# Another written order of the first group of an attention and MoE kernel

## The chip, the cores and the metric

One core of a Trainium2 chip. The metric is the device time of one execution, in microseconds (us), lower is better. The engines are TensorE (PE, with its weight loads PEld), VectorE (DVE), ScalarE (ACT), GpSimd (POOL) and SyncE (SP, which here only issues DMAs); each runs its own instructions in order, and they meet through semaphores.

## The reference, cut to what matters

Attention over 4 batches, 8 heads, 576 positions and 64 columns a head, half of the heads with a plain window of 32, half with a window of 128 at stride 4; then two MoE-like blocks on the 2304 tokens.

```python
scores = scale * q @ k.T            # per batch and head, then masked by window
attn = exp(scores - max) / sum
x = (attn @ v)                      # -> 2304 tokens x 512
h = x @ w_in                        # 512 -> 2048
x = (h - tanh(h)) @ w_out           # 2048 -> 512
a, b = x @ w1, x @ w2               # 512 -> 1024
out = ((a * b) @ w3) @ w_out2       # 1024 -> 1024 -> 512
```

## The kernel before, in words

Every fp32 product is done as three products of a high part and a low part of each operand. The hidden dimension of the first MoE block is worked in four groups of 3, 4, 4 and 5 chunks of 128 columns; after it come w1, w2, w3 and the output. **The change touches only the first group**, in which attention, the conversion of the first weights and the first products of the MoE block are interleaved. Their order is one written string, `ORDER` (lines 49 to 69), which `first_group` (line 756) walks through word by word. Each word emits the instructions of one step on one engine (or one queue), so the string sets the order on every engine at once. The rest of the program is emitted by loops and is not in the string.

A word is a letter, a number, and for attention mostly a `p` (plain heads) or `d` (dilated heads). The number of an attention word is the unit, 0 to 11 (three units of 192 positions a batch). From unit 3 on some steps do both halves at once. The attention words, in the order in which one unit goes through them:

- `q` (load_q, line 425): two loads of k and q on SP, 576 to 608 KB a half; `v` (load_v, line 444): two or three loads, 384 KB a half.
- `s` (at_scores, line 480): TensorE, mask and 48 small products a half, each 32 columns wide on the output side (tile `s`).
- `M` (at_max, 522): VectorE, a maximum and a subtraction; `E` (at_exp, 533): ScalarE; `N` (at_norm, 537): VectorE, a sum (L541), an addition (L545) and a reciprocal (L546); `m` (at_mult, 548): GpSimd.
- `T` (at_T, 557): TensorE, three transposes (tile `t`, one PSUM buffer); `C` (at_Tcopy, 568): ScalarE, two copies (L574).
- `P` (at_pv, 579): TensorE, 24 products with v for a half, 64 columns wide on the output side (L592, tile `x`, two PSUM buffers); `X` (at_hi, 611): ScalarE, high part (L614); `L` (at_lo, 616): VectorE, low part (L619).

The weight words go through weights 0 to 13 in the order in which they are needed:

- `w`: a load of 512 KB on SP into the tile `st`, which has two buffers (so the load of weight n+2 is issued only when the steps of weight n are done with its buffer);
- `a` (cv_abs, 142): ScalarE, L144; `b` and `c` (cv_bits, 147): VectorE, two instructions each (L149, L153; L159, L162); `i` (cv_hi, 166): ScalarE, L167; `o` (cv_lo, 169): GpSimd, L170.

The words of the MoE block go through 24 steps (seven tiles of 256 tokens and one of 512, three chunks each), and step 24 of the next group: `h` (st_h, 652) is 12 products of TensorE into the one PSUM buffer `h`, `t` (tanh, ScalarE, L677), `g` (VectorE, L683, which frees that buffer), `G` (ScalarE, L690), `k` (GpSimd, L697), `y` (st_y, 709: 12 products of TensorE, L725), and after a tile's last `y` the copies out, `Y` on ScalarE and `Z` on VectorE. `h0` needs the first three plain units and the three dilated halves up to `L1d`. K prepares masks, Q closes the pools of attention.

So what sets the order of work around the change is the string alone, and behind it four in-order engines and one in-order queue (SP). A wait of one word on an engine holds all later words of that engine. Three tiles with few buffers tie them together: `st` (2), `h` (1) and `s` (1 from unit 3 on, freed by `M`).

```python
            if kind in of_rest:
                of_rest[kind](n)
            elif part in "pd":
                of_unit[kind](n, ("pd".index(part),))
            else:
                of_unit[kind](n)
```

Of the kernel before, what the change touches and what calls it, by code (L numbers as in the profile page):

```python
# [46 lines left out]


ORDER = """
w0 K0 K1 a0 b0 c0 q0p q1p q2p q0d q1d s0p s1p w1 M0p M1p E0p E1p s2p M2p N0p N1p m0p w2 q2d s0d E2p  # L50
M0d a1 v0p v1p v2p N2p v0d b1 m1p E0d T0p c1 m2p s1d C0p T1p C1p a2 M1d P0p T2p X0p P1p s2d E1d w3
L0p C2p X1p N0d N1d m0d T0d C0d P2p a3 m1d T1d b2 X2p L1p P0d M2d q3p q3d v1d b3 c2 C1d E2d X0d i0
i1 N2d L2p s3 L0d q4p P1d m2d X1d c3 v2d i2 T2d C2d L1d q4d w4 M3 o0 w5 h0 t0 P2d g0 E3 N3 X2d o1 h1
q5p s4 o2 i3 G0 t1 g1 o3 L2d v3p k0 h2 a4 y0 q5d G1 a5 t2 b4 k1 c4 g2 m3p i4 T3p C3p h3 t3 M4 b5 m3d
T3d E4 N4 C3d o4 y1 G2 v3d c5 k2 s5 P3p g3 m4p q6p P3d i5 q6d h4 T4p o5 M5 v4p G3 t4 y2 E5 m4d C4p
g4 h5 Z2 T4d N5 v4d X3p L3p C4d k3 X3d s6 P4p G4 L3d t5 M6 P4d Y2 m5p X4p X4d v5p q7p T5p C5p k4 y3
L4p m5d y4 q7d v5d g5 G5 L4d E6 T5d P5p X5p v6p q8p N6 s7 q8d L5p h6 M7 C5d t6 k5 m6p P5d T6p X5d
C6p m6d g6 h7 T6d G6 y5 k6 t7 C6d g7 h8 s8 G7 L5d E7 P6p Y5 N7 m7p Z5 m7d t8 v6d P6d q9p T7p w6 g8
M8 y6 a6 b6 c6 h9 k7 y7 G8 k8 q9d C7p v7p E8 s9 N8 w7 m8p m8d i6 t9 v7d g9 X6p L6p T7d q10p q10d h10
M9 X6d v8p G9 t10 g10 y8 P7p v8d L6d o6 C7d a7 P7d E9 T8p N9 m9p k9 b7 C8p X7p h11 T8d C8d s10 m9d  # L60
G10 k10 L7p Z8 P8p M10 Y8 v9p X7d t11 X8p T9p y9 y10 L7d g11 L8p h12 E10 G11 N10 k11 v9d q11p C9p
t12 P8d X8d g12 G12 P9p T9d h13 C9d y11 L8d m10p m10d c7 t13 g13 k12 Y11 q11d X9p G13 Z11 v10p L9p
h14 t14 g14 T10p C10p w8 i7 s11 M11 P9d X9d P10p a8 b8 T10d X10p h15 E11 C10d L9d N11 k13 t15 g15
y12 y13 v10d G14 h16 w9 o7 c8 a9 k14 G15 y14 m11p t16 m11d Y14 g16 T11p Z14 L10p h17 C11p v11p k15
G16 P10d T11d X10d t17 b9 g17 y15 L10d c9 C11d k16 G17 P11p v11d P11d X11p L11p X11d y16 k17 L11d Q0
i8 i9 h18 y17 w10 w11 a10 t18 g18 h19 b10 o8 Z17 t19 c10 G18 i10 h20 k18 w12 o9 g19 o10 a11 G19 h21
b11 h22 t20 g20 Y17 k19 c11 i11 y18 G20 a12 o11 b12 y19 c12 k20 w13 a13 t21 h23 g21 t22 G21 y20 Y20
h24 Z20 i12 k21 y21 g22 b13 G22 c13 t23 g23 o12 G23 i13 k22 y22 k23 y23 t24 o13 g24 G24 Y23 Z23 k24
"""


# [1106 lines left out]
```

## Time and profile before

| | us |
|---|---|
| median of 3 runs | 797.55 (797.42 to 799.08) |
| the profiled execution | 797.63 |
| its span (first to last instruction) | 795.8 |
| TensorE busy | 775.3 (97%) |
| VectorE busy | 543.9 (68%) |
| ScalarE busy | 293.2 (37%) |
| GpSimd busy | 157.7 (20%) |
| mean granted clock of TensorE | 0.998 |

How to read it: the span lies within the profiled execution's own time, 1.8 us less. TensorE is busy for almost all of the span; VectorE, the next, for two thirds. A busy TensorE is not one at its peak, since the ends of its instructions are modelled and small products take longer per column than large ones. The shares are averages over the whole span, while the change touches the first 140 us or so.

### The profile page before, as it was taken

What the parts mean: (1) busy time and instruction counts of PE and PEld (TensorE: products, weight loads), DVE (VectorE), ACT (ScalarE), POOL (GpSimd) and SP (SyncE); (2) the same over time, 40 slices, a digit from 0 to 9 for tenths busy, and PEclk for the clock granted to TensorE, in tenths of its full rate; (3) what the DMA queues carried; (4) which work ended last, traced back from release to release, by engine and by line L of the source; (5) the groups of instructions that cost most, each with busy time, mean ns of one, the idle gap of its engine ahead of it and who ended that gap; (6) DMA issues with size and microseconds to landing.
All of it is one profiled execution on the core that took longest, in us unless ns stands there. A gap on an engine that the chain in (4) does not pass through costs nothing.

```text
span 795.8 us, 14135 instructions
## 1 busy us (share of the span) xinstructions
PE 775.3 (97%) x5592; PEld 684.1 (86%) x5592; DVE 543.9 (68%) x909; ACT 293.2 (37%) x546; POOL 157.7 (20%) x153
## 2 busy tenths in 40 slices
PE   4899999999999999999999999999999999999998
PEld 2689999888889888888888898799988999899996
DVE  6886766678888779887888899854455444634431
ACT  3655665434444434444444443411132111311111
POOL 3462434300111001120021223211121111211111
PEclk9999999999999999999999999999999999999999
DMA  9978752115454355533363343396203750166302
GB/s 322 317 227 249 235 187 81 53 55 170 144 171 136 85 166 146 172 107 104 114 193 103 99 157 107 108 350 198 85 22 95 242 186 0 40 191 202 112 1 79
DMA packets 60866, 115.58 MB, mean 145 GB/s; under 512 B 6272, under 2 KB 25856, under 8 KB 60800
## 3 DMA queue, kind: packets, MB, share of 16 engines
q1 hardware_dynamic: 60512, 114.32, 45.6%
q8 instruction: 44, 0.72, 0.4%
q10 hardware_dynamic: 288, 0.36, 0.2%
q14 instruction: 22, 0.18, 0.1%
HBM read 95.26 MB, written 19.40 MB: 144 GB/s over the span
## 4 chain that ended last, share of the span: by engine, by line
PE 88%; DVE 7%; DMA 3%; ACT 1%; issue 1%; SPq 0%; ACTq 0%; DVEq 0%
PE h L635 26%; PE y L725 25%; PE pr L979 22%; PE o L1042 6%; PE pr L1042 5%; PE x L592 2%; DVE a L159 1%; PE s L508 1%; DVE a L162 1%; DMA v<-in_vt 1%; PE t L561 1%; DMA Y<-in_kT 1%; DMA out<-o 1%; DVE a L153 1%; DVE Y L872 1%
## 5 line engine op out<-in xcount | busy, mean ns | idle before, releaser
L725 PE MATMUL y<-gs,LT 128*128 128x512 f32 (+1 forms) x520 | 121.9, 368 | 0.0
L725 PEld LDWEIGHTS y<-gs,LT 128*128 128x128 f32 x520 | 92.1, 188 | 16.3
L635 PE MATMUL h<-X,LT 128*128 128x512 f32 (+1 forms) x471 | 104.9, 370 | 0.0
L635 PEld LDWEIGHTS h<-X,LT 128*128 128x128 f32 x471 | 82.8, 188 | 15.2
L683 DVE TENSOR_TENSOR th<-h,th 128x512 f32<-128x512 f32 (+1 forms) x83 | 51.2, 616 | 55.2 <-ACT th L677 55.1
L979 PE MATMUL pr<-X 128*128 128x384 f32 x435 | 82.1, 335 | 0.0
L979 PE MATMUL pr<-X,LT 128*128 128x384 f32 x405 | 81.0, 336 | 0.3 <-ACT u L1019 0.3
L677 ACT ACTIVATE th<-h 128x512 f32<-128x512 f32 (+1 forms) x83 | 44.7, 540 | 93.6 <-PE h L635 88.7
L635 PE MATMUL h<-X,w 128*128 128x512 f32 (+1 forms) x381 | 78.7, 352 | 0.0
L979 PEld LDWEIGHTS pr<-X 128*128 128x128 f32 x435 | 76.2, 188 | 0.8 <-DVE v L1016 0.3
L159 DVE SCALAR_TENSOR_TENSOR a<-st,a 128x512 uint32<-128x512 uint32 x68 | 74.5, 1095 | 0.4
L979 PEld LDWEIGHTS pr<-X,LT 128*128 128x128 f32 x405 | 71.9, 188 | 1.9 <-ACT u L1019 0.6
L1016 DVE TENSOR_TENSOR u<-pr,u 128x384 f32<-128x384 f32 x72 | 40.1, 557 | 46.8 <-PE pr L979 38.4
L635 PEld LDWEIGHTS h<-X,w 128*128 128x128 f32 x381 | 62.7, 188 | 10.2
L690 ACT ACTIVATE gs<-th 128x512 fp32r<-128x512 f32 (+1 forms) x83 | 47.8, 576 | 62.6 <-DVE th L683 56.9
L725 PE MATMUL y<-gs,w 128*128 128x256 f32 (+1 forms) x352 | 70.0, 328 | 0.0
L144 ACT ACTIVATE a<-st 128x512 f32<-128x512 f32 x68 | 45.7, 673 | 61.7 <-DMA st<-in_w 21.7
L992 ACT ACTIVATE cs<-u 128x384 fp32r<-128x384 f32 x24 | 12.6, 526 | 148.5 <-DVE u L1016 148.5
L1034 POOL TENSOR_TENSOR Y<-w,v 128x384 f32<-128x384 f32 x24 | 24.5, 1020 | 213.7 <-DVE w L1016 213.7
L725 PEld LDWEIGHTS y<-gs,w 128*128 128x128 f32 x352 | 54.5, 188 | 6.4
L170 POOL TENSOR_TENSOR LT<-a,LT 128x512 fp32r<-128x512 f32 x18 | 24.5, 1367 | 153.7 <-ACT LT L167 153.7
L162 DVE SCALAR_TENSOR_TENSOR a<-st,a 128x512 uint32<-128x512 uint32 x68 | 51.5, 757 | 2.3
(169 smaller groups left out, 1252.8 us busy)
## 6 DMA issues: line engine op xcount, KB each, us to landing
st<-in_w SPq DMA_DIRECT2D x28, 512.0 KB, 3.5
LT<-p SPq DMA_DIRECT2D x56, 256.0 KB, 4.5
X<-p SPq DMA_DIRECT2D x56, 256.0 KB, 5.0
st<-in_w_in SPq DMA_DIRECT2D x16, 512.0 KB, 4.2
st<-in_w_out SPq DMA_DIRECT2D x16, 512.0 KB, 4.2
v<-in_vt SPq DMA_DIRECT2D x40, 192.0 KB, 4.5
q<-in_qz SPq DMA_DIRECT2D x18, 384.0 KB, 4.9
p<-LT SPq DMA_DIRECT2D x26, 256.0 KB, 4.5
```

Source lines behind the costliest of these rows:

```text
L144: nc.scalar.activation(out=a.bitcast(F32), in_=st[:, :, 1].bitcast(F32), func=ACTF.Abs)
L159: nc.vector.scalar_tensor_tensor(out=a, in0=st[:, :, 1], scalar=0xC0000000, in1=a, op0=ALU.bitwise_and, op1=ALU.bitwise_or)
L162: nc.vector.scalar_tensor_tensor(out=a, in0=st[:, :, 0], scalar=29, in1=a, op0=ALU.logical_shift_right, op1=ALU.bitwise_or)
L170: nc.gpsimd.tensor_tensor(out=lo, in0=a.bitcast(F32), in1=hi.bitcast(F32), op=ALU.subtract)
L635: nc.tensor.matmul(out=ps, lhsT=a[sel[0]], rhs=b[sel[1]], start=(start and i == 0), stop=(i == n - 1), **kw)
L677: nc.scalar.activation(out=th[:, :tn], in_=gst[i][:, :tn], func=ACTF.Tanh)
L683: nc.vector.tensor_tensor(out=th[:, :tn], in0=ps[:, :tn], in1=th[:, :tn], op=ALU.subtract)
L690: nc.scalar.activation(out=gs[:, 0, :tn], in_=th[:, :tn], func=ACTF.Copy)
L725: nc.tensor.matmul(out=y[k], lhsT=wt[sel[0]][:, 128 * k:128 * k + 128], rhs=gs[:, sel[1], tn * m:tn * m + tn], start=(cs[m] == 0 and n == ...
L979: nc.tensor.matmul(out=ps[:, :TP], lhsT=s[e][:, 128 * k:128 * k + 128], rhs=(hi, lo)[f][1][k], start=start and n == 0, stop=n == 5, skip_g ...
L1016: nc.vector.tensor_tensor(out=out, in0=ps[:, :TP], in1=x, op=op)
L1042: nc.tensor.matmul(out=tiles[m], lhsT=cs[e][:, 128 * m:128 * m + 128], rhs=WW[j][f], start=begin and n == 0, stop=end and n == 2,)
```

## The change

`ORDER` holds the same 504 words before and after, each once, in another order; nothing else in the file changes. In the new order the second weight (`w1`) is loaded directly behind the first q and k, the third (`w2`) ahead of the last two dilated halves, and the fourth (`w3`) ahead of the first v, where it stood behind four halves of v. The steps of the weights move on the engines with them. Ten times two halves of products with v (`P`) stand side by side on TensorE, where there were seven.

```diff
@@ -47,25 +47,25 @@
 ORDER = """
-w0 K0 K1 a0 b0 c0 q0p q1p q2p q0d q1d s0p s1p w1 M0p M1p E0p E1p s2p M2p N0p N1p m0p w2 q2d s0d E2p
-M0d a1 v0p v1p v2p N2p v0d b1 m1p E0d T0p c1 m2p s1d C0p T1p C1p a2 M1d P0p T2p X0p P1p s2d E1d w3
-L0p C2p X1p N0d N1d m0d T0d C0d P2p a3 m1d T1d b2 X2p L1p P0d M2d q3p q3d v1d b3 c2 C1d E2d X0d i0
-i1 N2d L2p s3 L0d q4p P1d m2d X1d c3 v2d i2 T2d C2d L1d q4d w4 M3 o0 w5 h0 t0 P2d g0 E3 N3 X2d o1 h1
-q5p s4 o2 i3 G0 t1 g1 o3 L2d v3p k0 h2 a4 y0 q5d G1 a5 t2 b4 k1 c4 g2 m3p i4 T3p C3p h3 t3 M4 b5 m3d
-T3d E4 N4 C3d o4 y1 G2 v3d c5 k2 s5 P3p g3 m4p q6p P3d i5 q6d h4 T4p o5 M5 v4p G3 t4 y2 E5 m4d C4p
-g4 h5 Z2 T4d N5 v4d X3p L3p C4d k3 X3d s6 P4p G4 L3d t5 M6 P4d Y2 m5p X4p X4d v5p q7p T5p C5p k4 y3
-L4p m5d y4 q7d v5d g5 G5 L4d E6 T5d P5p X5p v6p q8p N6 s7 q8d L5p h6 M7 C5d t6 k5 m6p P5d T6p X5d
-C6p m6d g6 h7 T6d G6 y5 k6 t7 C6d g7 h8 s8 G7 L5d E7 P6p Y5 N7 m7p Z5 m7d t8 v6d P6d q9p T7p w6 g8
-M8 y6 a6 b6 c6 h9 k7 y7 G8 k8 q9d C7p v7p E8 s9 N8 w7 m8p m8d i6 t9 v7d g9 X6p L6p T7d q10p q10d h10
-M9 X6d v8p G9 t10 g10 y8 P7p v8d L6d o6 C7d a7 P7d E9 T8p N9 m9p k9 b7 C8p X7p h11 T8d C8d s10 m9d
-G10 k10 L7p Z8 P8p M10 Y8 v9p X7d t11 X8p T9p y9 y10 L7d g11 L8p h12 E10 G11 N10 k11 v9d q11p C9p
-t12 P8d X8d g12 G12 P9p T9d h13 C9d y11 L8d m10p m10d c7 t13 g13 k12 Y11 q11d X9p G13 Z11 v10p L9p
-h14 t14 g14 T10p C10p w8 i7 s11 M11 P9d X9d P10p a8 b8 T10d X10p h15 E11 C10d L9d N11 k13 t15 g15
-y12 y13 v10d G14 h16 w9 o7 c8 a9 k14 G15 y14 m11p t16 m11d Y14 g16 T11p Z14 L10p h17 C11p v11p k15
-G16 P10d T11d X10d t17 b9 g17 y15 L10d c9 C11d k16 G17 P11p v11d P11d X11p L11p X11d y16 k17 L11d Q0
-i8 i9 h18 y17 w10 w11 a10 t18 g18 h19 b10 o8 Z17 t19 c10 G18 i10 h20 k18 w12 o9 g19 o10 a11 G19 h21
-b11 h22 t20 g20 Y17 k19 c11 i11 y18 G20 a12 o11 b12 y19 c12 k20 w13 a13 t21 h23 g21 t22 G21 y20 Y20
-h24 Z20 i12 k21 y21 g22 b13 G22 c13 t23 g23 o12 G23 i13 k22 y22 k23 y23 t24 o13 g24 G24 Y23 Z23 k24
+w0 K0 K1 q0p w1 a0 s0p a1 q1p q2p q0d b0 c0 i0 s1p M0p b1 E0p N0p c1 M1p s2p M2p m0p E1p w2 q1d N1p
+q2d s0d M0d T0p E2p N2p o0 C0p m1p a2 w3 s1d s2d v0p v1p v2p v0d E0d N0d q3p a3 q3d m2p T1p P0p C1p
+M1d X0p m0d E1d b2 P1p T2p N1d C2p T0d c2 X1p w4 L0p i1 L1p C0d m1d v1d M2d v2d b3 P2p i2 X2p E2d
+q4p P0d L2p T1d X0d s3 N2d q4d m2d c3 o1 C1d P1d L0d X1d T2d v3p L1d a4 C2d M3 h0 b4 t0 q5p E3 g0 G0
+N3 o2 w5 c4 P2d k0 s4 q5d h1 y0 X2d m3p i3 t1 g1 T3p o3 a5 v3d h2 M4 q6p i4 o4 G1 L2d C3p s5 t2 g2
+m3d P3p E4 G2 X3p b5 T3d v4p h3 k1 N4 m4p m4d y1 q6d C3d T4p M5 L3p t3 C4p c5 v4d E5 s6 P3d g3 q7p
+G3 k2 P4p i5 T4d X3d X4p C4d h4 o5 N5 t4 w6 m5p q7d M6 m5d E6 y2 k3 g4 L3d T5p v5p L4p Z2 v5d C5p h5
+T5d P4d s7 X4d N6 t5 q8p L4d m6p C5d v6p M7 P5p Y2 m6d P5d g5 T6p q8d X5p v6d L5p y3 h6 w7 C6p G4
+T6d s8 X5d E7 N7 G5 k4 a6 C6d L5d P6p t6 m7p m7d P6d M8 g6 T7p a7 X6p k5 y4 h7 L6p E8 t7 N8 y5 q9p
+G6 Z5 X6d k6 g7 C7p Y5 q9d L6d m8p s9 v7p v7d T7d b6 h8 C7d t8 q10p P7p P7d T8p G7 X7p b7 g8 X7d L7p
+h9 y6 k7 y7 q10d L7d v8p v8d t9 m8d M9 E9 C8p g9 h10 G8 N9 c6 k8 c7 m9p T8d G9 s10 C8d P8p t10 P8d
+T9p X8p g10 w8 q11p y8 a8 h11 Y8 L8p v9p Z8 k9 t11 g11 y9 m9d h12 G10 C9p M10 G11 k10 k11 t12 g12
+E10 y10 N10 h13 G12 X8d w9 m10p t13 y11 g13 T9d C9d h14 a9 G13 q11d Y11 m10d b8 k12 Z11 v9d L8d t14
+s11 M11 P9p X9p L9p P9d X9d E11 v10p k13 v10d T10p g14 c8 N11 C10p y12 y13 G14 T10d L9d m11p h15 w10
+v11p P10p C10d t15 P10d T11p g15 b9 h16 m11d X10p v11d C11p k14 L10p T11d X10d t16 G15 k15 g16 L10d
+c9 y14 C11d P11p Y14 G16 X11p Z14 k16 i6 P11d X11d L11p i7 h17 L11d t17 y15 Q0 h18 g17 h19 t18 o6
+G17 g18 y16 k17 i8 a10 w11 b10 y17 i9 c10 w12 Z17 G18 k18 i10 t19 g19 G19 h20 h21 o7 o8 h22 a11 o9
+b11 k19 Y17 a12 t20 t21 o10 y18 g20 g21 G20 y19 k20 G21 b12 c11 c12 i11 h23 y20 t22 Y20 Z20 g22 k21
+t23 h24 w13 G22 a13 g23 i12 y21 G23 b13 k22 c13 y22 o11 t24 k23 g24 o12 i13 y23 Z23 Y23 G24 k24 o13
 """
```

## Rows read from the trace of the kernel before

**Rows 1.** Busy time by stretch: stretch, length, then busy (x instructions), clock, DMA.
```profile
0.00:60.00 60.00, 44.11 (x1064) 37.59 (x1064) 46.85 (x90) 32.36 (x67) 28.00 (x39) 0.97 0.89 289
...
60.00:140.00 80.00, 80.00 (x1297) 74.91 (x1292) 54.19 (x100) 48.21 (x106) 31.04 (x35) 1.00 0.60 186
...
140.00:500.00 360.00, 360.00 (x1735) 303.02 (x1735) 299.94 (x485) 153.17 (x263) 58.33 (x44) 1.00 0.42 126
```

**Rows 2.** The chain of waits, 0 to 62 us: start, length, what.
```profile
11.24 9.16 DMA v<-in_vt
...
23.98 0.44 DVE ms L541
...
44.86 1.70 PE h L635 x12
```

**Rows 3.** Waits of TensorE, 5 to 45 us: waiter, releaser, total, times, longest.
```profile
PE h L635 <- DVE th L683: 1.4, 2, 1.0
```

**Rows 4.** Timeline of VectorE and GpSimd: start, length, instruction, idle before.
```profile
24.45 0.53 DVE L545 TENSOR_SCALAR ms<-ms 128x6 f32<-128x6 f32 x1
...
25.12 0.38 DVE L149 TENSOR_SCALAR a<-a 128x512 f32<-128x512 f32 x1
...
25.54 0.93 DVE L153 TENSOR_SCALAR a<-a 128x512 uint32<-128x512 uint32 x1
...
26.40 0.55 DVE L619 TENSOR_TENSOR X<-x,X 128x384 fp32r<-128x384 f32 x1
...
29.43 0.69 DVE L162 SCALAR_TENSOR_TENSOR a<-st,a 128x512 uint32<-128x512 uint32 x1
...
32.56 1.65 DVE L162 SCALAR_TENSOR_TENSOR a<-st,a 128x512 uint32<-128x512 uint32 x1
...
34.14 0.55 DVE L619 TENSOR_TENSOR X<-x,X 128x384 fp32r<-128x384 f32 x1
...
34.61 0.94 DVE L526 TENSOR_REDUCE ms<-s 128x12 f32<-128x768 f32 x1
...
35.65 0.96 DVE L529 TENSOR_TENSOR pm<-s,ms 128x768 f32<-128x768 f32 x1
...
38.47 1.29 POOL L170 TENSOR_TENSOR w<-a,w 128x512 fp32r<-128x512 f32 x1 [1.87 <-ACT w L167]
...
38.51 1.27 DVE L545 TENSOR_SCALAR ms<-ms 128x12 f32<-128x12 f32 x1
```

**Rows 5.** Timeline of ScalarE, 22 to 28 us.
```profile
22.40 0.52 ACT L535 ACTIVATE pm<-pm 128x384 f32<-128x384 f32 x1
...
24.25 0.49 ACT L614 ACTIVATE X<-x 128x384 fp32r<-128x384 f32 x1 [0.30 <-PE x L592]
...
25.86 1.05 ACT L574 ACTIVATE pb<-t,sel_sb 128x384 f32<-128x384 f32 x2 [1.11 <-PE t L561]
...
27.04 0.67 ACT L144 ACTIVATE a<-st 128x512 f32<-128x512 f32 x1
```

**Rows 6.** Landing time in us of two loads, issued at 10.65 and 22.72.
```profile
Y<-in_qz SPq DMA_DIRECT2D x1, 384.0 KB, 9.2
...
st<-in_w_in SPq DMA_DIRECT2D x1, 512.0 KB, 4.3
```

**Rows 7.** Busy time by stretch again, two short ones of the fill.
```profile
16.00:17.00 1.00, 0.64 (x28) 0.48 (x27) 0.88 (x4) 0.13 (x1) 0.00 (x0) 1.00 1.09 373
...
21.00:22.00 1.00, 1.00 (x20) 0.88 (x18) 0.18 (x1) 0.15 (x1) 0.00 (x0) 0.50 0.60 181
```

**Rows 8.** The chain of waits, 44 to 104 us.
```profile
50.12 1.55 PE x L592 x48
...
51.66 1.62 PE h L635 x12
...
55.03 1.42 PE h L635 x12
...
68.09 0.85 PE x L592 x24
```

## The prediction

> **What bounds the kernel now.** I first read the busy time by stretch, to see where TensorE has any room. From 60 to 140 us and from 140 to 500 us it is busy for every microsecond; in the first 60 us for only 44.11, so 15.9 us are missing there [rows 1]. All 504 words of the order lie in the first 140 us or so, and TensorE's work is the same before and after. The change can therefore win only part of those 15.9 us, or what TensorE loses between unlike products, and it can lose if it opens a wait after 60 us.
>
> The chain of waits then says what ends last inside the fill. Up to 20.4 us it runs through loads (the last one a load of v, issued at 11.24); from 22.5 us on it is one VectorE step after another, until TensorE takes over for good with the `h3` products at 44.86 [rows 2]. So the place to argue is: when does VectorE get through the steps that the first MoE products need, and does TensorE wait again behind them? The waits of TensorE show 1.4 us in two waits of `h` for a `g` on VectorE, the last of them right before 44.86 [rows 3].
>
> **The change part by part: the fill up to L1d.** `h0` needs `L1d`, the last low part of the first units; before, that step ends at 34.14 + 0.55 = 34.69 [rows 4]. Up to it VectorE does the same steps in both orders, and so does TensorE. Only their order and their waits differ.
>
> *The loads moved.* The second weight passes q1p, q2p and q0d in SP's queue. At 373 GB/s (a stretch with the transfers full, [rows 7]) its 512 KB take 1.4 us, so those q land 1.4 us later. That is covered: VectorE now has the second weight's b and c to do between the first units' maxima, where before it had to wait for products. The third weight passes only q1d and q2d; SP holds there until `c0` frees the first buffer, with the first q's still queued in front, so the transfers don't run dry. The last q of the fill lands at 10.65 + 9.2 = 19.85 as before [rows 6], because the bytes up to it are the same. Then comes the fourth weight, now ahead of v: 19.85 + 1.4 = 21.3 us. The first v follows at 22.35 (384 KB more), against 20.4 before [rows 2]: `P0p` is 1.9 us late.
>
> *Who stands behind them.* ScalarE's queue now reads a3, C1p, X0p, E1d. `a3` waits for the fourth weight, so after 21.3 come 0.67 (a) and 1.05 (C); `P0p` is done at 22.35 + 0.85 = 23.2 [rows 8]; then X 0.49 and E 0.52 [rows 5] give 24.2, with small gaps 24.3 us. On VectorE `N1d` waits for that E1d, with everything up to L1d behind it. Before, N1d began at 23.98 [rows 2]. I estimate that VectorE reaches N1d some 2.4 us earlier and idles.
>
> *From N1d to L1d.* Before, this stretch takes 34.69 - 23.98 = 10.7 us. In the new order it holds the same steps but for two: b2 is already done (25.12 to 26.40, 1.3 us off), and L0p comes in (about 0.5 us) [rows 4]. That makes 9.9 us with the delays of before, among them one c instruction of 1.65 against 0.69 us, beside GpSimd's low parts o0 to o2. In the new order o0 has run long before and o1, o2 come after m2d, so I take half of that 0.96 off: 9.4 us, with 8.9 and 9.9 as ends. L1d ends at 24.3 + 9.4 = 33.7 us: **1.0 us earlier** (0.5 to 1.5). What else could be last there is P1d: its v stands behind the fifth weight, which SP issues after `c2`, at about 26.4 us (N and c behind 24.3). With 4.3 us to land [rows 6], 1.1 for the v, 0.85 for P and 0.49 for X, this comes to 33.1, just as L1d can start. So it costs nothing, but there is no cover behind it: what makes c2 later makes L1d later.
>
> [...]
>
> **After L1d.** TensorE runs h0, P2d, s4, h1, y0, T3p, h2 then. The two waits of 1.4 us [rows 3] should go, as s4 now stands between h0 and h1 and covers `g0`. Two new ones come. First, `s5` follows h2 directly, and the scores tile is freed by `M4`, which stands on VectorE right behind the `g1` that releases h2: M4 takes two passes like 0.94 and 0.96 [rows 4], h2 takes 1.42 [rows 8], so s5 waits 0.5 us. Second, `c4` now stands ahead of g1, with GpSimd's o3 beside it; VectorE's L545 took 1.27 us beside such an o of 1.29 [rows 4], and the c above was 0.96 longer. Between 0 and 1.0 us I take 0.3, since y0 lies between h1 and h2 (12 products like an h, 1.42 us) and covers the rest. Balance: -1.4 + 0.5 + 0.3 = **-0.6 us** (-1.2 to +0.1).
>
> [...]
>
> **The dense part.** A lone P takes 0.85 us and a pair 1.55, so each run of P costs 0.15 us beyond its products; an h behind a P takes 1.62 instead of 1.42 [rows 8]. Counted in the two orders from s5 to h18, runs of P go from 11 to 10 and changes from narrow products (s, P) to wide ones from 12 to 10: 0.15 + 2 x 0.2, **-0.5 us** (-0.3 to -0.6). I looked in the new order for waits that TensorE would meet there (each h for the g before it, T for the one transpose buffer, P for the L two back, s for the q that its predecessor frees, the first y of a tile for Y and Z) and found each releaser ahead by the lengths above. The cover is VectorE's slack, 54.2 us busy of 80 [rows 1]. Behind the first group nothing is moved; the words for the last weights end at the same step, so I cost that at nothing.
>
> **Sum.** -1.0 - 0.6 - 0.5 = -2.1 us on the profiled 797.63 (span 795.8 and 1.8 around it) is 795.5; that execution lies 0.1 above the median, so 795.4. The ends: -1.5 - 1.2 - 0.6 = -3.3 (794.3) and, with the half clock, +0.35 + 0.1 - 0.3 = about 0 (797.7).
>
> **The rivals.** A difference of 0.2% (1.6 us) is about what a measurement can tell from no change.
>
> *Same work, same time.* VectorE does the same set of steps before L1d, and what it no longer waits for at the start it waits for at N1d; a P at half clock and a blocked c4 then eat the rest, and only the dense part's 0.5 us is left: 797.0. For it: N1d starts no earlier than before. Against it: b2 lies before N1d now. Chance 0.25.
>
> *Slower: ScalarE stands behind the fourth weight.* The place is a3 ahead of C1p, X0p and E1d. Its load can go out only when `c1` frees the second weight's buffer, by the lengths above about 13.4 us; the longest landing of the fill, 9.2 us [rows 6], puts it at 22.6, and 1.3 us more if o0 blocks c1 [rows 4], 23.9. Each microsecond behind 21.3 moves N1d, L1d and h0. From a landing at 23.4 on the gain is gone; from 25.0 on it is slower by over 0.2%. At 23.9, with P at half clock (0.85) and no balance left from the waits (0.6): -2.1 + 2.6 + 0.85 + 0.6 = +1.95, 799.5. Against it: the bytes ahead of this load are the same as those ahead of the last q. Chance 0.11.
>
> *More than forecast.* The transfers ran dry before (181 GB/s at 21 to 22 us, [rows 7]), when SP had only small loads of v to issue; a weight of 512 KB ahead of them fills that hole. If all later loads come early too, c runs undisturbed and no new wait opens: -1.5 - 1.4 - 0.6 = -3.5, 794.0, or a little less. Chance 0.09.
>
> **How the numbers follow.** The forecast, 795.4 with its own range of 794.3 to 797.0, has 0.55; about 0.08 of that lies within 0.2%. Faster: 0.47 + 0.09 = 0.56; same: 0.25 + 0.08 = 0.33; slower: 0.11. The range goes from 793.9 to 798.4: it takes in most of the better case, all of the equal one, and leaves out the slower one and tails.
>
> **What would show it.** Right: the first v lands near 22.4 and a3 ends near 22; N1d starts near 24.3 after an idle VectorE; L1d ends at 33.2 to 34.2; TensorE is gapless from about 44 us, with one gap of some 0.5 us at s5; pairs of P in the dense part at 1.55 us. Wrong: a3 later than 23; a wait of TensorE behind 60 us; L1d after 34.7; or P at half clock before L1d.

## The result, and the profile after

The changed kernel takes **802.89 us** (median of 5 runs, 801.85 to 805.05) against 797.55 before: a ratio of 1.0067, 95% interval 1.0056 to 1.0078. It is slower by 5.3 us, where I had forecast 2.1 us less. The profiled execution, the longest of the five, took 805.05 us with a span of 803.3, 7.5 more than the span before.

The busy time by stretch answers [rows 1]:

```profile
0.00:60.00 60.00, 41.98 (x1006) 34.77 (x1007) 42.44 (x86) 30.00 (x61) 27.26 (x38) 0.94 0.93 305
60.00:140.00 80.00, 79.16 (x1307) 74.92 (x1307) 53.56 (x97) 48.19 (x109) 29.60 (x33) 0.98 0.54 167
140.00:500.00 360.00, 360.00 (x1748) 303.64 (x1747) 297.89 (x484) 153.25 (x264) 60.06 (x46) 1.00 0.42 127
```

From 140 to 500 us TensorE is busy throughout in both. In the first 60 us TensorE has done 58 products fewer than before, and from 60 to 140 us its clock is below 1.00. Finer stretches of the same view show where:

```profile
50.00:52.00 2.00, 2.00 (x55) 1.51 (x57) 2.00 (x3) 0.94 (x2) 1.47 (x3) 1.00 0.85 216
52.00:54.00 2.00, 1.77 (x92) 1.54 (x80) 1.93 (x5) 1.73 (x5) 0.00 (x0) 1.00 1.06 381
54.00:56.00 2.00, 0.00 (x0) 0.00 (x0) 1.19 (x3) 0.43 (x2) 1.87 (x2) 1.00 1.04 383
56.00:58.00 2.00, 0.51 (x10) 0.54 (x12) 0.00 (x0) 0.00 (x0) 1.65 (x3) 0.61 0.92 321
58.00:60.00 2.00, 2.00 (x25) 1.88 (x22) 0.03 (x1) 0.52 (x2) 0.00 (x0) 0.50 0.11 34
60.00:62.00 2.00, 2.00 (x11) 2.00 (x11) 0.92 (x1) 1.02 (x2) 0.00 (x0) 0.50 0.75 203
62.00:64.00 2.00, 2.00 (x14) 2.00 (x13) 1.05 (x3) 1.12 (x2) 0.00 (x0) 0.68 0.90 288
```

92 products in 52 to 54 us, then none at all in 54 to 56 us while the transfers are full (383 GB/s), and then a granted clock of 0.50 for some 6 us. TensorE's timeline gives the place, `P4p` (the second run of 24 here), and the chain of waits what it names as the reason:

```profile
52.85 0.92 PE L592 MATMUL x<-pb,v 128*64 128x64 f32 x24
57.49 1.55 PE L592 MATMUL x<-pb,v 128*64 128x64 f32 x24 [3.72 <-DMA st<-in_w_in]
58.97 0.90 PE L561 MATMUL t<-id_sb,pm 128*128 128x128 f32 x3
...
67.17 0.50 PE L496 MATMUL s<-mask_sb,id_sb 128*128 128x384 bf16 x2
```

```profile
50.43 6.55 DMA st<-in_w_in
56.99 0.50 issue
57.49 1.55 PE x L592 x24
```

That name is no operand: `P4p` reads `pb` and `v`, not the sixth weight. The changed kernel's page has, in its part on the DMA queues, a line of a kind that I had passed over, and a line of busy totals that fits it:

```profile
PE 779.4 (97%) x5592; PEld 687.6 (86%) x5592; DVE 543.7 (68%) x909; ACT 292.7 (36%) x546; POOL 157.9 (20%) x153
...
q8 instruction: 44, 0.72, 0.4%
```

44 packets with 0.72 MB (packets, MB, share): over TensorE's 2 x 5592 instructions that is 64 bytes each and 254 of them a packet of 16 KB. So TensorE's own program comes in pieces, through the same transfer engines as the data, of whose time it takes 0.4%. The view of the DMA queues by single microseconds shows one such packet in 54 to 55 us in the changed kernel, and in 52 to 53 us in the kernel before (packets, MB, share of that microsecond):

```profile
q8 instruction: 1, 0.02, 6.5%
```

```profile
q8 instruction: 1, 0.02, 5.8%
```

**Theory F**: `P4p` is the first work of a new piece, and its packet was still behind the data. Busy time from the start counts how far TensorE was, first in the changed kernel, then in the one before:

```profile
0.00:53.80 53.80, 39.47 (x977) 32.34 (x977) 41.05 (x82) 28.85 (x58) 23.73 (x34) 0.97 0.95 311
```

```profile
0.00:53.60 53.60, 37.71 (x893) 31.62 (x894) 42.38 (x80) 27.09 (x55) 25.01 (x35) 0.97 0.89 291
...
0.00:57.90 57.90, 42.01 (x982) 35.59 (x986) 45.23 (x87) 30.40 (x62) 26.43 (x37) 0.97 0.89 290
```

The changed kernel stops behind 977 products and 977 weight loads. The kernel before comes to that count only at about 57.8 us, some 5 us behind its packet. The expectations below name the same place "instruction 1985", since TensorE's whole queue also holds instructions that the page does not count as busy, 31 up to there in the trace. Counted with these, the three stops of this kind in the two profiles stand behind 1985 and 2753 instructions (changed) and 449 (before): three and six times 256 apart.

### The profile page after: what moved, and what is told of

The parts are those of the page before. It is cut to its first block, busy times and chain, and to the rows that moved or that the text cites. A ratio compares the mean times of both kernels' runs of the same rounds, so it can differ in the third digit from the quotient of the medians.

```text
span 803.3 us, 14144 instructions
## 1 busy us (share of the span) xinstructions
PE 779.4 (97%) x5592; PEld 687.6 (86%) x5592; DVE 543.7 (68%) x909; ACT 292.7 (36%) x546; POOL 157.9 (20%) x153
## 4 chain that ended last, share of the span: by engine, by line
PE 88%; DMA 4%; DVE 4%; issue 1%; ACT 1%; SPq 1%; ACTq 0%
PE h L635 26%; PE y L725 25%; PE pr L979 21%; PE o L1042 6%; PE pr L1042 5%; PE x L592 2%; PE s L508 2%; DMA st<-in_w_in 2%; DVE a L159 1%; PE t L561 1%; DMA Y<-in_qz 1%; DMA q<-in_qz 1%; DMA out<-o 1%; DVE a L162 1%; DVE Y L872 1%
## 5 line engine op out<-in xcount | busy, mean ns | idle before, releaser
L979 PE MATMUL pr<-X 128*128 128x384 f32 x435 | 82.1, 335 | 0.0
L979 PE MATMUL pr<-X,LT 128*128 128x384 f32 x405 | 81.0, 336 | 0.7 <-ACT u L1019 0.7
L979 PEld LDWEIGHTS pr<-X 128*128 128x128 f32 x435 | 76.2, 188 | 0.8 <-DVE v L1016 0.3
L979 PEld LDWEIGHTS pr<-X,LT 128*128 128x128 f32 x405 | 71.8, 188 | 2.3 <-ACT u L1019 1.0
```

What stands on the lines that cost most here:

```text
L979: nc.tensor.matmul(out=ps[:, :TP], lhsT=s[e][:, 128 * k:128 * k + 128], rhs=(hi, lo)[f][1][k], start=start and n == 0, stop=n == 5, skip_g ...
```

## The experiments

All runs compare with the kernel before on the same chip (797.25 to 797.41 us there).

**The change again.**

> The changed kernel again. Its trace shows TensorE idle from 53.8 to 57.5 us ahead of the second of two products with v (P4p), and its clock at one half from 57.4 to 64 us. Theory F (the fetch): TensorE has run out of instructions and waits for the next 16 KB of its program, which it shares the transfer engines with; the stall is then a matter of timing and may be smaller or larger in another execution, with 3 to 5 us of spread in the time. Theory L (the load): P4p waits for the weight load whose landing the trace puts ahead of it (the seventh weight); the stall is then there every time, 3.5 to 4 us long. Time by both 801 to 805.

802.1 us (two executions; ratio 1.0059, 1.0039 to 1.0079); the wait ahead of `P4p` was 2.61 us, at 977 products again, where Theory L had 3.5 to 4 every time.

**Another cause of the same place: two small loads.** In the changed kernel's trace `P4p` waits on one of eight semaphores that count landings, and both a load of `v` (issued at 43.62 us) and the sixth weight's (50.43 us) count that one up. Two 8 KB loads into a spare tile, behind `q6d`, shift all later landings in that count.

```diff
-m4p m4d y1 q6d C3d T4p
+m4p m4d y1 q6d D0 D1 C3d T4p
```

> The changed order with two small loads (8 KB each, read by nobody) written between the two loads of q6d and the two of v4d, so that every later load signals on another of SP's eight landing signals than before; P4p then shares its two signals with the loads of q7p, which land near 55 us, and no longer with the seventh weight. Bytes in flight are the same. Theory L: the stall at P4p ends at about 55 us, 1 to 1.5 us long, time near 799. Theory F: the stall stays, 2 to 4 us long, and the time is 801 to 805.

801.41 us (1.005, 1.0032 to 1.0069; single executions from 797.14 to 804.37). In the profiled execution (804.37) the wait stays at 977 products, and the name goes (waits of TensorE, 50 to 62 us), so the named load was no cause:

```profile
PE x L593 <- issue: 2.9, 1, 2.9
```

**Moving the program against the work.** Tiny products ahead of `s0p`, where TensorE has nothing to do (its first 6.40 us), put 16 and 128 instructions ahead of the rest. The word `J64` emits 64 of them, `J8` 8:

```diff
+nc.tensor.matmul(out=ps[:32, :16], lhsT=warm[:, :32], rhs=warm[:, :16], start=True, stop=True)
...
-w0 K0 K1 q0p w1 a0 s0p a1
+w0 K0 K1 q0p w1 a0 J64 s0p a1
```

> The same with 8 tiny products (16 instructions). Theory F: the wait stays, 2.5 to 3.5 us, but moves 16 instructions (8 products) earlier in the work: it falls inside the run of 24 small products of P3d, with its last 8 behind the wait, though all 24 read the same tiles; time 801 to 804. Rivals: the wait stays where it was, ahead of P4p's first product, at 2.5 to 3.8 us, with the same time.

801.83 us (1.0055, 1.0042 to 1.0068). The wait moved by 8 products to the earlier side, into the middle of `P3d`. Behind 16 of its 24 products TensorE stands still, then come the other 8 and the 24 of `P4p`:

```profile
52.71 0.69 PE L593 MATMUL x<-pb,v 128*64 128x64 f32 x16
55.53 1.98 PE L593 MATMUL x<-pb,v 128*64 128x64 f32 x32 [2.14 <-issue]
```

The 8 read no tile, and no load of `v`, that the 16 had not read already. This is the run that decides for F, though its wait of 2.14 us is 0.4 shorter than F expected.

> The changed kernel with 64 tiny products (32x16, 128 instructions of TensorE with their weights) written ahead of s0p, where TensorE has nothing to do until 6.2 us; the order is otherwise that of the change. Theory F (TensorE's program comes in 16 KB pieces of 256 instructions by the same transfer engines as the data, and the piece that starts with P4p is not there yet): the borders of the pieces move by half a piece against the work, the piece that ends near P4p then holds long products beside the short ones, and the wait of 2.6 to 3.8 us ahead of P4p goes (under 0.5 us), or a smaller one (under 1.5 us) stands half a piece away; the time is 797 to 799. Rivals (the sixth weight's load, or any tile that P4p reads, is late): the wait ahead of P4p stays at 2.5 us or more, time 801 to 804.

798.63 us (797.55 to 801.91; 1.002, 1.001 to 1.003). In TensorE's timeline (of an execution of 797.58) the wait ahead of `P4p` is gone, `P3d` and `P4p` run as one row of 48, and the clock stays at 1.00. A shorter wait stands in `s7`, three products from its end:

```profile
52.92 1.62 PE L593 MATMUL x<-pb,v 128*64 128x64 f32 x48
54.47 0.55 PE L562 MATMUL t<-id_sb,pm 128*128 128x128 f32 x3
...
60.69 0.50 PE L497 MATMUL s<-mask_sb,id_sb 128*128 128x384 bf16 x2
61.12 1.53 PE L509 MATMUL s<-k,q 128*32 128x64 f32 x93
63.51 0.30 PE L509 MATMUL s<-k,q 128*32 128x64 f32 x3 [0.86 <-issue]
```

This also prices the low clock. From the transposes behind `P4p` to `s7` the changed kernel took 67.17 - 58.97 = 8.2 us, here it is 6.2 for the same work; with `P4p` itself at 1.55 in place of half of 1.62, the low clock cost 2.7 us.

The next run was aimed at that second wait, and badly: `s7`, where it stands, comes ahead of the word that I moved.

```diff
-M7 P5p Y2 m6d P5d g5 T6p q8d X5p v6d L5p y3 h6
+M7 Y2 P5p m6d y3 P5d g5 T6p q8d X5p v6d L5p h6
```

> The run with 64 tiny products ahead of s0p, and with y3 (12 long products) moved between P5p and P5d, its eviction Y2 ahead of P5p. There TensorE waited 0.9 us with nothing but issue named, at instruction 2497, again 193 and a multiple of 256. Theory F: the piece of program that ends there takes 1.4 to 1.6 us longer, so this wait goes (under 0.3 us): time 796.6 to 798.0, and the slowest of its executions come nearer to the median (801.9 before). Rival (that wait was a one-off or has another cause): the time stays at 798.6.

798.7 us; the wait stands where it stood (behind 1229 products in both runs). It tells nothing of the rival.

**The same wait made in the kernel before.**

```diff
-w0 K0 K1 a0 b0 c0 q0p q1p q2p q0d q1d s0p s1p
+w0 K0 K1 a0 b0 c0 q0p q1p q2p q0d q1d J48 s0p s1p
```

> The kernel before with 48 tiny products (96 instructions) ahead of s0p. Theory F: the borders move so that 256 instructions that TensorE went through in 2.5 us (s6 and P4p with most of P4d, 57 to 60 us) make one piece of the program; a wait of 0.3 to 2 us appears inside P4d, 18 instructions from its end, unless the next piece, asked for at the start of s6, gets through the transfers (0.83 to 0.93 busy there) within 2.5 us; time 797.5 to 800. Rivals (the wait belongs to the changed order's data): no wait in P4d, time 797 to 798.

800.1 us (1.0045, 1.003 to 1.0059), 0.1 above the range. TensorE's timeline has a wait inside `P4d`, 8 products from its end, as expected; the waits over the whole span show four among products with v, the longest 1.6 us, inside `P10p`. Three of them stand inside a row of products (the fourth, 0.22 us, at the start of `P1d`). The longest wait of this kind is another, which I had not expected: 2.17 us in the fill, inside `s0d`, behind 221 products, with a granted clock of 0.50 from 16 to 19 us behind it:

```profile
15.38 0.65 PE L508 MATMUL s<-Y 128*32 128x64 f32 x23 [2.17 <-issue]
...
58.13 1.39 PE L592 MATMUL x<-pb,v 128*64 128x64 f32 x40
60.06 0.45 PE L592 MATMUL x<-pb,v 128*64 128x64 f32 x8 [0.55 <-issue]
```

```profile
PE x L592 <- issue: 2.7, 4, 1.6
```

Inside `P4d` it stops behind 1104 products, the run with 64 behind 1229, the changed kernel behind 977: steps of 127 and 125 products, with their weight loads some 250 instructions, one packet.

> The kernel before with 88 tiny products (176 instructions) ahead of s0p. The shortest piece of its program up to 110 us then takes TensorE 4.35 us by its own trace, in place of 3.4 us without them and 2.5 us with the 48 that made three waits. Theory F: no wait for instructions over 0.3 us, time 796.8 to 797.8, as the kernel before (797.3) or a little under. Rival (tiny products ahead of the work cost time by themselves, by their number, the clock or the first pieces of program): 799.5 or more, as with 48.

798.25 us (1.0017, 1.0008 to 1.0026): 0.8 us slower than the kernel before, which neither side expected, though with 88 no wait for instructions is left behind 34 us. TensorE's timeline shows two in the fill, inside `s2p` and inside `P1d`:

```profile
13.76 0.42 PE L508 MATMUL s<-Y 128*32 128x64 f32 x14 [1.37 <-issue]
...
33.82 0.69 PE L592 MATMUL x<-pb,v 128*64 128x64 f32 x16 [1.21 <-issue]
```

They stand behind 221 and 600 products, that is 756 and 377 ahead of 977, six and three packets of 126 products with their weight loads. So the borders cost in the fill too; I had looked only at the pieces behind it. In the run with 64 tiny products there is one of 1.07 us in `s2d`, behind 348 products, five packets ahead of 977.

**The early load of the sixth weight.** First taken back in the changed kernel (`w6` ahead of `w7`, `a6` ahead of `a7`), then put alone into the kernel before.

```diff
-C4d h4 o5 N5 t4 w6 m5p q7d M6
+C4d h4 o5 N5 t4 m5p q7d M6
```

> The changed order with the seventh weight's load and its first step (w6, a6) moved back beside those of the eighth. 0.5 MB less is in flight at 50 to 57 us. Theory F: the packet of TensorE's program gets through earlier, the stall at P4p goes or shrinks under 1.5 us, the clock stays up, time 796.5 to 799. Theory L: the load that P4p waited for is gone from there, so the stall goes as well unless the next load on its place takes over (then it lasts until the next q lands, 1 to 4 us).

800.06 us (1.0034, 1.0023 to 1.0045), 1.1 above the range of F. In the profiled execution (798.86) the wait shrinks to 1.24 us at the same place, with another name, and the clock stays at 1.00 there; a wait of 0.96 us for instructions inside `s1d`, behind 220 products, and one of 1.23 us in `s5` for `q5d` stand ahead of it:

```profile
55.63 0.92 PE L592 MATMUL x<-pb,v 128*64 128x64 f32 x24 [1.24 <-DMA k<-in_kT]
```

```diff
-m4p q6p P3d i5 q6d h4 T4p
+m4p q6p P3d i5 q6d w6 h4 T4p
```

> The kernel before with one part of the change alone: the sixth weight's load w6 (512 KB) moved ahead of the fifth's values, behind q6d, so that it starts at about 50.4 us as it does in the changed kernel, in place of 69.9 us; its ScalarE copy a6 stays. Theory F: the early load lengthens the queues of the transfers and brings the piece of program for instruction 1985 (52.6 us in the kernel before) up to 2 us later, but TensorE comes to that instruction only at 57.9 us there, so there is no wait: time 797.0 to 798.2. Rival (the early load alone makes the loss, by taking the bandwidth from the queries, keys and values): a wait of 1 us or more for a transfer between 52 and 66 us, time 798.5 to 801.

797.85 us, ratio 1.0005 (0.9996 to 1.0014): no difference, with the load starting at 50.54 us and no wait of TensorE from 44.9 to 140 us (in the fill one for instructions, 0.86 us in `s3`, behind 472 products). Here the early load costs nothing measurable. In the changed kernel, where the packet that `P4p` needs stands behind it, the wait was 3.72 us, and 1.24 with the load late.

**Making the piece last longer.** 12 long products, 24 instructions, go into the row of short ones, `y1` in one run and `h4` (with `g3`, which frees its bank, earlier, and the sixth weight late again) in another.

```diff
-N4 m4p m4d y1 q6d C3d T4p M5 L3p t3 C4p c5 v4d E5 s6 P3d
+N4 m4p m4d q6d C3d T4p M5 L3p t3 C4p c5 v4d E5 s6 y1 P3d
```

> The changed kernel with the second product of the second pair of blocks, y1, written behind s6 and ahead of P3d in place of ahead of T4p. Theory F: 12 long products (1.4 us) and their weights move into the piece of program that ends at P4p, so that the border falls 24 instructions earlier, inside P3d, and the next piece has 1.4 us longer to come: the wait shrinks by 1.2 to 1.6 us against the unchanged order of the change (2.6 to 3.8 us), to 1 to 2.5 us, and stands inside P3d; time 799.5 to 801.5. Rivals: the wait stays ahead of P4p; since TensorE has the same work ahead of it, it stays as long (2.6 to 3.8 us), time 801 to 804.

801.52 us (1.005, 1.0038 to 1.0062). The wait for instructions is gone, but both theories missed what came: without `y1` ahead of it, `T4p` waits for `m4p`, and a granted clock of 0.50 (52 to 54 us) follows, so that `s6` takes 2.79 in place of 1.55 us:

```profile
50.38 0.55 PE L561 MATMUL t<-id_sb,pm 128*128 128x128 f32 x3 [1.52 <-POOL pm L551]
51.29 0.48 PE L496 MATMUL s<-mask_sb,id_sb 128*128 128x384 bf16 x2 [0.36 <-DVE pm L529]
51.70 2.79 PE L508 MATMUL s<-k,q 128*32 128x64 f32 x96
```

```diff
-L3p t3 C4p c5 v4d E5 s6 P3d g3 q7p G3 k2 P4p i5 T4d X3d X4p C4d h4 o5
+L3p t3 g3 C4p c5 v4d E5 s6 h4 P3d q7p G3 k2 P4p i5 T4d X3d X4p C4d o5
```

> The changed kernel with the sixth weight's load and copy back ahead of the seventh's, and h4 (12 long products, 24 instructions) moved between s6 and P3d, the subtraction g3 that frees its bank ahead of C4p. No tiny products. Theory F: the piece of program from instruction 1729 to 1985 then holds h4 in place of half of P3d and takes TensorE 1.1 to 1.3 us longer (h4 1.55 to 1.7 for 24 instructions that took 0.4), so the wait of 1.24 us that was left with the sixth weight late goes (under 0.3 us), or stands under 0.5 us inside P3d; with s5's wait of 1.0 to 1.2 us still there, time 796.5 to 798.5. Rival (that wait was k's or another tile's transfer, as the view names it): it stays at 1 us or more ahead of P4p, time 799.5 to 800.5.

799.1 us (1.0024, 1.0012 to 1.0035), 0.6 above the expected range. The wait fell from 1.24 to 0.46 us and moved by the 12 products that were put in; three more for instructions stand in its fill (0.96, 0.56 and 0.72 us, behind 220, 471 and 597 products):

```profile
53.99 0.57 PE L592 MATMUL x<-pb,v 128*64 128x64 f32 x12
55.02 1.27 PE L592 MATMUL x<-pb,v 128*64 128x64 f32 x36 [0.46 <-issue]
```

**What became of the fill's gain.** `w4` behind `q4d`, its steps later too:

```diff
-c2 X1p w4 L0p i1 L1p C0d m1d v1d M2d v2d b3 P2p i2 X2p E2d q4p P0d L2p T1d X0d s3 N2d q4d m2d
+c2 X1p L0p i1 L1p C0d m1d v1d M2d v2d b3 P2p i2 X2p E2d q4p P0d L2p T1d X0d s3 N2d q4d w4 m2d
```

> The changed order with the fifth weight's load moved back behind q4d and its steps behind it (a4 after t1, b4 and c4 after M4). This is about the fill alone: in the changed kernel P1d waits 0.8 us for its v and s4 waits for q4d until 39.05 us, both behind this load. If the load is what ate the gain of the fill, P1d starts by 31.7 instead of 32.40, s4's second half by 38.0, and h3 1 to 1.5 us earlier than at 47.6; if VectorE is what bounds the fill, h3 comes within 0.5 us of 47.6. The stall at P4p may come or go with the timing; the time says little, 797 to 804.

802.17 us (1.0058, 1.0035 to 1.008). `s4` no longer waits and h2 ends at 43.11 in place of 44.69 us, but then `s5` waits 1.1 us for `q5d`, `P3p` 0.67 for ScalarE, and h3 starts at 48.14 (47.59 in the changed kernel); the wait ahead of `P4p` stays, 3.2 us. In this profile, what one transfer gains, the next lacks.

The two halves of the orders were also crossed: the new fill (up to `h2`) with the old rest, and the old one (up to `h3`) with the new rest.

> The change's order as far as h2 (its first 45 us), and behind it all that is left in the order of the kernel before. The border of TensorE's program at its instruction 1729 and 1985 then falls in the old rest, as it does in the kernel before, within 2 instructions. Theory F with the forecast's fill: no wait of over 0.7 us for instructions, and the fill's gain alone stays: TensorE's 7 steps up to h2 end at 43.0 to 44.7 us and h3 starts 0.5 to 1.5 us sooner than in the kernel before (44.86); time 795.8 to 797.0. Rival (the fill gains nothing on the whole, as in the changed kernel's profiled run): 797.2 to 798.0. Rival (the loss sits in the fill): 799 or more.

797.89 us (1.0014, 1.0004 to 1.0023). No wait for instructions stands behind 31 us, but there are two in the fill, 0.94 us in `s1d` and 0.21 in `s3` (behind 220 and 471 products), where F had none of over 0.7. My expectation of a gain fell too: h3 starts at 44.67 against 44.86 [rows 2], since it waits for the `g` on VectorE as before:

```profile
18.26 0.64 PE L508 MATMUL s<-Y 128*32 128x64 f32 x28 [0.94 <-issue]
...
44.67 1.57 PE L635 MATMUL h<-X,WG 128*128 128x256 f32 x11 [0.99 <-DVE th L683]
```

> The counterpart: the kernel before's order up to h3, behind it all that is left in the order of the change. Theory F: TensorE's instruction 1985 is again within a few of P4p's first product, with the same short products ahead of it and the same transfers beside it: a wait of 1.5 to 3.8 us there, then some microseconds at clock 0.5; time 801 to 804, as the changed kernel or 1 us over it. Rival (the wait comes from how the new fill leaves the queues): no such wait, time 797 to 799.

799.81 us (1.0032, 1.0022 to 1.0042). Here F's number failed, and the rival's 797 to 799 too: no wait of over 0.3 us ahead of `P4p`. TensorE had lost 2.35 us ahead of `s5` and then ran at the low clock (0.50 from 48 to 50 us), so it came to `P4p` at about 56 us, while its packet passed in 53 to 54 us.

```profile
45.47 0.50 PE L496 MATMUL s<-mask_sb,id_sb 128*128 128x384 bf16 x2 [2.35 <-DMA v<-in_vt]
```

Two versions were meant to beat both kernels, by taking away `s5`'s wait for `q5d`. The first has 64 tiny products, `w6` late and `w5` behind `q5d`; the second, in place of the tiny products, `h4` early as above, and ScalarE's `a5` moved too (the diff shows the second).

```diff
-N3 o2 w5 c4 P2d k0 s4 q5d h1 y0 X2d m3p i3 t1 g1 T3p o3 a5 v3d h2 M4 q6p i4 o4 G1 L2d C3p s5 t2 g2
+N3 o2 c4 P2d k0 s4 q5d w5 h1 y0 X2d m3p i3 t1 g1 T3p o3 v3d h2 M4 q6p i4 o4 G1 L2d C3p s5 t2 a5 g2
```

> A version that might beat both: the changed kernel with 64 tiny products ahead of s0p, the sixth weight's load and copy back ahead of the seventh's (as in an earlier run), and the fifth weight's load behind the other q of that unit (q5d), for which s5 waited 1.0 to 1.2 us in several executions. Theory F and the sum of the parts seen: no wait for instructions ahead of P4p, s5's wait gone; 798.6 of the run with 64 tiny products, less 0.9 to 1.2 for s5 where it waited: 796.6 to 798.0. Rival (what is gained at s5 is given back at the fifth weight's conversion, which h3 or y2 then waits for): 798.0 to 799.5.

801.18 us (1.0043, 1.003 to 1.0055): the rival's side, and worse than it. `a5` now waits 4.4 us for its load, `C3p` stands behind it on ScalarE, `P3p` waits 2.21 us for that, and `h3` behind it takes 2.81 us (1.67 at a clock of 1.00 in the run with the sixth weight late). Two waits for instructions stand in it as well, 1.50 us in `s2d` and 1.38 in `h7` (behind 348 and 1481 products):

```profile
48.51 0.92 PE L593 MATMUL x<-pb,v 128*64 128x64 f32 x24 [2.21 <-ACT pb L575]
49.41 0.55 PE L562 MATMUL t<-id_sb,pm 128*128 128x128 f32 x3
49.72 2.81 PE L636 MATMUL h<-X,WG 128*128 128x256 f32 x12
```

> The same, with the fifth weight's load behind q5d and, other than in the run with three edits, its ScalarE copy a5 moved too, from T3p to behind t2, so that C3p and P3p don't stand behind the transfer. If s5's wait for q5d is what takes the fill's gain: that wait goes (1.0 to 1.2 us), time 795.5 to 797.3, under the kernel before. Rival (the wait moves on to the next step whose data are not there, since TensorE is ahead of VectorE and the transfers there): 797.3 to 799.

798.73 us (1.0017, 1.0008 to 1.0027). `s5` waits no more, but the wait for instructions is back at 1.21 us, at the same 977 products: the fifth weight's 512 KB now fill the transfers ahead of the packet (369 GB/s in 48 to 50 us, against 337 in the run before it).

```profile
55.28 1.27 PE L592 MATMUL x<-pb,v 128*64 128x64 f32 x36 [1.21 <-issue]
```

No version beats the kernel before.

**All profiles on one scale.** The trace has every packet's start. The third column is the time at which TensorE begins the piece that ends at 977 products (its 852nd product):

| run | wait at 977 | piece begun | packet starts | next product |
|---|---|---|---|---|
| changed kernel | 3.72 | 50.35 | 54.79 | 57.49 |
| the same again | 2.61 | 50.74 | 54.69 | 57.30 |
| two small loads | 2.90 | 52.04 | 56.54 | 59.09 |
| `w4` late | 3.16 | 50.90 | 55.59 | 58.20 |
| 8 tiny products | 2.14 | 48.82 | 52.94 | 55.53 |
| `w6` late | 1.24 | 50.25 | 53.11 | 55.63 |
| `h4` early, `w6` late | 0.46 | 50.03 | 52.66 | 55.02 |
| the same, `w5` late | 1.21 | 49.46 | 52.98 | 55.28 |
| kernel before | none | 50.74 | 52.60 | 57.84 |
| kernel before, `w6` early | none | 50.78 | 53.04 | 57.88 |

In the eight profiles with a wait at this border the next product starts 2.3 to 2.7 us after the packet does, whether the wait is 0.46 or 3.72 us, so the packet is what TensorE waited for. In the first five rows, with the sixth weight early, the packet comes 4.0 to 4.7 us after the start of the piece, in the next three, with it late, 2.6 to 3.5, and in the old order 1.9 and 2.3. (With `y1` behind `s6` and the sixth weight early it took 1.3, so that weight is not all of it.) And over the first 140 us of all 18 profiles, the kernel before among them (0.36 us in `s1d`), TensorE stops 30 times for 0.2 us or more within products of one line with "issue" named; each time the count of products lies within 2 of 977 plus or minus a multiple of 126.

## Why the prediction was wrong

**N1d, right.** The first v, `a3` and N1d came where the working put them: `P0p` at 22.28 (22.35), a3 from 21.27 (21.3), N1d at 24.27 (24.3). One reading of the queue was off: the second weight passes q1d as well, and the third passes q1d alone (it stood ahead of q2d before). The bytes up to the last q are the same, so the times did not suffer.

**L1d, 1.0 us earlier: wrong by all of it.** VectorE and ScalarE, answering [rows 4, 5], and TensorE:

```profile
24.27 0.55 DVE L541 TENSOR_REDUCE ms<-pm 128x6 f32<-128x384 f32 x1 [2.53 <-ACT pm L535]
...
25.85 1.20 DVE L162 SCALAR_TENSOR_TENSOR a<-st,a 128x512 uint32<-128x512 uint32 x1
...
31.80 1.20 DVE L162 SCALAR_TENSOR_TENSOR a<-st,a 128x512 uint32<-128x512 uint32 x1
...
34.19 0.56 DVE L619 TENSOR_TENSOR X<-x,X 128x384 fp32r<-128x384 f32 x1 [0.72 <-ACT X L614]
```

```profile
33.66 0.49 ACT L614 ACTIVATE X<-x 128x384 fp32r<-128x384 f32 x1 [2.74 <-PE x L592]
```

```profile
32.40 1.22 PE L592 MATMUL x<-pb,v 128*64 128x64 f32 x24 [0.77 <-DMA v<-in_vt]
...
39.05 0.88 PE L508 MATMUL s<-k,q 128*32 128x64 f32 x48 [0.48 <-DMA q<-in_qz]
```

L1d ends at 34.75 (34.69 before), 10.5 us behind N1d where I took 9.4. Two terms of that step were mis-sized. Both c's took 1.20 us, not 0.69, so I should not have taken half of that surcharge off. And the path that I costed at nothing, P1d's v behind the fifth weight, ended last: X1d was done at 34.15 in place of 33.1, for c2 ended at 27.05 (26.4), `P1d` could start only at 32.40, and it took 1.22 us where I had 0.85. "No cover behind it" was the right warning, with a price of zero beside it. The 0.85 us for a P at half clock, in the slower end of the sum and in a rival, no run shows: in the kernel before a P at a granted clock of 0.50 (at 22.73 us) took 1.48 us, 0.56 more than the 0.92 of `P0p` here, and here the 0.50 (19 to 22.3 us) met `s1d`, `s2d` and `T1p`, and no P.

**After L1d, -0.6 us: the waits went as said, the balance did not come.** The two waits of `h` are gone. The 0.5 us that I gave to `s5` behind `M4` did not come. But `s4` waited 0.7 us for `q4d` (0.23 and, in the row above, 0.48): in the new order that load stands behind one weight more, and I had followed v into the queue but not the q behind it. h2 ended at 44.69, and by the chain the next step began there, 0.2 us sooner than h3 before [rows 2]. `c4`'s second instruction, which stands in a rival as blocked, did take 1.20 us (39.93 to 41.13) beside GpSimd's work (39.52 to 42.29), but no product waited for it.

**The dense part: the step that failed.** "I looked in the new order for waits that TensorE would meet there ... and found each releaser ahead." Each releaser *was* ahead; I had counted only what semaphores release. TensorE also needs its own program, and this order brings three things together: T4p, s6 and P3d, 125 short products that with their weight loads use up just one packet of instructions, in 3.3 us (50.47 to 53.77); the border of the piece right behind them; and the sixth weight, queries and values that fill the transfers at 381 to 383 GB/s. Of the 7.5 us of span, 3.72 are this wait, 2.7 the low clock that followed, and 0.70 a second wait of the same kind at 77 us (behind 1354 products, three packets after 977). The remaining 0.4 stand at 619 us, where the products of tile `pr` (L979) wait 0.68 us for ScalarE, against 0.29 before. The expected -0.5 us from fewer changes between narrow and wide products no run showed by itself.

The rivals missed it too: the one on the slow side had its place at `a3`, which was on time. The range ended at 798.4, the slower side had 0.11.

All 44 packets have 16,384 bytes. From 140 us on 26 start in the changed kernel and 25 in the one before, each within 42 instructions of TensorE's passing a border (449 plus a multiple of 256). By their count a packet is the one for the next border, so in these traces a piece is all the time that its successor has to come. Two of the 44 here came too late behind the fill (3.72 and 0.70 us).

**What stays open.** Whether the changed order would beat the one before if no border hurt it: the run with 64 tiny products is 1.3 us above the kernel before, with 1.07 and 0.86 us of such waits left in its profile, though that profiled execution (797.58) is as long as the kernel before's (797.63). The one run of the changed order whose profile shows none of them (`y1` behind `s6`) lost 1.52 us to `m4p` and then the low clock. That the fill's gain is taken by the next load (`q5d`) or by VectorE's `g` is shown in single profiles only. Executions of the changed order spread further (797.14 to 804.37 with the two small loads) than those of before (796.24 to 799.38 over all chips); that this is the packet's luck among the data was argued, not shown.

## What to carry to other kernels

Where TensorE runs through hundreds of short products next to full transfers (here 92 in 2 us, beside 381 GB/s), count its instructions too: find the "instruction" line of the DMA queues (q8 here, 44 packets), divide (254 instructions a packet here), and ask where the borders fall and how many microseconds each piece lasts. Here a piece that lasted 3.3 us beside full transfers cost 3.7 us and a low clock (0.50) behind it; a large load moved away shortened the wait to 1.24 us, and 12 long products among the short ones besides to 0.46. In these runs the sign was a wait with a name that the waiting instruction does not read (3.72 us, named for `st`), or with "issue" in the middle of a row of equal products (2.14 us inside `P3d`).

## What the runs showed that I had not expected

- Between the packet and the next product there is time as well, 2.3 to 2.7 us by the table above, of which the packet's own transfer takes 1.05 us in the changed kernel (0.88 to 1.84 over its 44 packets).
- The low clock is a second bill. Behind the fill it followed standstills of 2.14 to 3.72 us in seven profiles (a granted clock down to 0.50 to 0.57 in the slowest 2 us of five; in the runs with 8 tiny products and with three edits, transposes of 0.90 in place of 0.55 us and an `h3` of 2.81 in place of 1.67), and one of 1.52 us with 0.36 soon behind it, but not those of 0.46, 0.86, 1.21, 1.24 and 1.38 us, nor one of 1.57 in the kernel before with 48 tiny products (whose 2.17 us in the fill it did follow). The 3.72 us brought 2.7 more.
- Tiny products, run where TensorE had nothing to do, cost time by where they put the borders: 88 made the kernel before 0.8 us slower, with stops of 1.37 and 1.21 us, 48 of them 2.7 us, with stops of up to 2.17.
